# Linear attention and a rational FFN on one core: the first block of each batch as one chunk, the weight conversion's sign ahead of its shift, another order

## The chip, the cores and the metric

The kernel runs on one NeuronCore of a Trainium2 chip. PE (TensorE) does the matmuls, DVE (VectorE), ACT (ScalarE) and POOL (GpSimd) the elementwise work; SP (SyncE) issues all transfers between HBM and SBUF here. PE writes to PSUM, from where DVE and ACT read; POOL works on SBUF alone. The metric is the device time of one execution in microseconds, as the median of several runs. Beside it stands one profiled execution, whose trace gives start and duration of every instruction.

## The reference

The first half is a linear attention with a decaying state over 4 batches, 8 heads, 768 tokens and a head of 48; the second half is a feed-forward layer over 3072 tokens (384 to 2048 to 384) with a rational activation:

```python
for t in range(S):
    kt, vt, rt = (k[:, :, t], v[:, :, t], r[:, :, t])
    cur = np.einsum('bhd,bhe->bhde', u[None] * kt, vt)
    y[:, :, t] = np.einsum('bhd,bhde->bhe', rt, state + cur)
    state = w[None, :, :, None] * state + np.einsum('bhd,bhe->bhde', kt, vt)
...
h = x @ w_in
P = a[0] + a[1] * h + a[2] * h2 + a[3] * h3
Q = 1.0 + np.abs(b[0]) * np.abs(h) + np.abs(b[1]) * h2
return ((P / (Q + 1e-06)) @ w_out).astype(np.float32)
```

The decays w are drawn from 0.85 to 0.95. The FFN's weights come as 64-bit floats.

## The kernel before

**Attention.** The 24 blocks of 128 tokens are numbered n = 0 to 23; block n belongs to batch n % 4, so blocks 0 to 3 are the first of their batches. r and k are scaled with powers of the decay, so that the recurrence becomes matmuls. The scaling is centred on the middle of the block. For each block:

- "Lk", "Lr", "Lv" load, "sk" and "sr" scale; "ba", "bb", "bs", "bv" make the bonus term of u
- "tk" and "tr" transpose k and r on PE, "tke" and "tre" copy the results out of PSUM on ACT ("tre" in two halves)
- "a" (lines 542 to 551) makes the scores: the block is cut into two chunks of 64 tokens, and heads sit in pairs on the two row halves of the array, so that 64 × 64 matmuls alternate between the halves; "ae" applies the causal mask on DVE and puts the scores into the free half of the transposed r
- "kv" (564 to 575) makes the sums of k times v, once over the first 64 tokens and once over all 128; "kve" adds the state to them on DVE (for a first block, where there is none, it copies them on ACT)
- "LV" copies (ACT, DVE) or loads (SP) v into the state tile vs, beside the state, so that "y" (590 to 600) gets scores times v and r times state from one matmul of 128 rows and 64 columns of weights
- "ca" multiplies the state with the decay for the next block, "ye" adds the bonus, "x" transposes, "xh" and "xl" split the result into a high and a low FP32R part

**Weights.** The 28 pieces of w_in and w_out are loaded as integers ("cl"). ACT scales the top words ("c0") and the low words ("cu"); DVE shifts the scaled top words by 3 into a PSUM tile ("c2") and then puts the sign of the unshifted words on ("c3"); POOL adds the low word ("cr"); ACT rounds to the high part ("ch"), and POOL or DVE makes the low part ("co").

**FFN.** The hidden layer of 12 pairs of blocks is worked off in 50 slices, nearly all of four hidden tiles of 256 tokens. "f1" makes a slice (9 matmuls per hidden tile), ACT and DVE evaluate the activation ("z", "q", "t", "ln", "ex" on ACT, "u3", "hi", "p", "d", "lo" on DVE), "f2" multiplies with w_out, "os" evicts and "od" stores.

**Order.** All instructions of all engines are issued in the sequence of a long string, ORDER, written out by hand or by a search; a token names task, block or slice, engine and buffer (tke.0A: the copy of block 0's transposed k on ACT). Each engine works off its own tokens in that order. "warm" tokens are fill: matmuls of a constant tile with itself, whose result is not used:

```python
o_ = ops[max(ops)][1] if ops else idle_bank
nc.tensor.matmul(o_[:, DM:512], wones, wones, start=alone, stop=alone)
```

A test of the inputs at the end (the decays within W_MIN and W_MAX, among others) decides whether a slow general path runs behind the fast one.

Of the kernel before, what the change touches and what calls it, by code (L numbers as in the profile page):

```python
# [48 lines left out]
ORDER = """
pad.1G coefS wS Lv.2S plG uwS st0.1G st0.0G Lv.3S Lk.0S idG pad.0G pad.2G Lr.2S cl_D Lr.1S betaA sqD Lr.0S Lk.2S Lk.1S mskG ctrA  # L50
st0.3G st0.2A LV.1.1.1A LV.1.0.1A LV.1.0.0A LV.1.1.0A ubG warm.65P ubpPpa0 ubeA pow.0D turn.0.0Ppa1 pow.1D inv.1D pow.2D inv.2D
warm.20P turn.2.0P inv.0D wlD turn.1.0P tab.0A sr.1G sr.2D sr.0D warm.28P turn.0.1Ppa0 turn.1.1P turn.2.1P tab.1A sk.2D sk.0D
ba.2Dm0 ba.0Dm1 wpPpa1 w128A bb.2D sk.1G bs.2D bv.2D bb.0D tr.1Ph0 tre.1.0A tre.1.1A ba.1Gm2 bb.1G warm.16P tk.0Ppa0 tke.0A cl.2S
cu.2A c0.2A c2.2Dh1 c3.2D cr.2Gta0 Lv.0S cl.5S bs.0D bv.0G tr.0Ppa1 tre.0.1A tre.0.0A Lr.3S sr.3G kv.2Ph0 kve.2.0A kve.2.1A Lv.1S
kv.0Ppa0 Lk.3S sk.3G kve.0.0A kve.0.1A warm.14P a.0Ppa1 tk.1Ph1 tke.1A ae.0.1D ae.0.0D c0.5A c2.5Dh0 c3.5D warm.16P a.1Ph1
warm.10P tk.2Ph0 ae.1.0D ae.1.1D ch.2A co.2D LV.0.0.1A LV.0.1.0A LV.0.0.0A ba.3Dm3 bb.3D LV.0.1.1A warm.24P y.0Ph1 ca.0.0G ca.0.1G
cl.6S cu.6A c0.6A c2.6Dpa0 c3.6D cr.6Gta1 cl.12S cu.12A c0.12A tke.2A c2.12Dh0 Lr.4S sr.4G tr.2Ppa1 tre.2.1A tre.2.0A cl.1S c0.1A
bs.1D bv.1G Lk.5S cl.26S warm.17P kv.1Ppa0 kve.1.0A kve.1.1A Lk.4S kv.3Ppa1 kve.3.1A kve.3.0A cu.26A c3.12D cr.12Gta2 sk.5G ye.0D
warm.2P x.0Ph0 xh.0A bs.3D c2.1Dh1 c3.1D a.2Ppa0 tk.3Ppa1 tke.3A ae.2.1D ae.2.0D sk.4D y.1Ph1 tr.3Ppa1 ca.1.1D ca.1.0D ye.1D cu.5A
cr.5Gta3 xl.0D ba.4Dm1 bb.4G y.2Ppa0 ye.2D warm.37P x.2Ppa0 ch.12A Lr.5S sr.5G tre.3.1A c0.26A c2.26Dh1 c3.26D cu.1A cr.1Gta4  # L60
# [108 lines left out]
def tile_linear_attention_rational_ffn(ctx, tc, r, k, v, w, u, w_in, w_out, a, b, out):  # L169
# [65 lines left out]
    def pro_load():  # L235
        tab["zero"] = at.tile([P, P], F32, tag="os", name="zero", bufs=NO)
        nc.gpsimd.memset(tab["zero"], 0.0)
        nc.gpsimd.memset(identw, 0.0)
# [2 lines left out]
        nc.gpsimd.memset(wones, 1.0)
# [694 lines left out]
```

## Time and profile before

| | |
|---|---|
| median of 3 runs | 569.54 us (568.47 to 569.60) |
| profiled execution | 568.78 us, its span 567.1 us |
| PE / PEld busy | 550.2 / 528.6 us |
| DVE / ACT / POOL busy | 473.0 / 393.2 / 160.2 us |
| granted TensorE clock | 0.996 |

PEld is PE's weight load, which overlaps the matmuls. The span runs from the first to the last instruction; the time of an execution also holds what lies around it. A row of instructions names line, engine, operation, "output<-inputs" and the shape. "A <- B" in a view of waits says that A's engine sat idle until B was done. A matmul in FP32 appears as two instructions of PE.

### The profile page before, as it was taken

How to read it: one execution, taken by the hardware profiler on the slowest of the kernel's cores; microseconds unless marked ns; L12 is line 12 of the kernel's file. 1: busy time of each engine (PE TensorE's matmuls, PEld its weight loads, DVE VectorE, ACT ScalarE, POOL GpSimd, SP SyncE). 2: the span in 40 equal slices, each digit the busy share in tenths (PEclk: the TensorE clock that was granted, in tenths of full speed). 3: DMA queues.
4: the chain of work that ended last, by engine and by line, in shares of the span. 5: the costliest groups of instructions: out<-in, count | busy, mean ns of one | idle time of the engine just before them, and what ended most of it. 6: DMA issues, size and time to landing. Idle time of an engine off the chain costs nothing.

```text
span 567.1 us, 13844 instructions
## 1 busy us (share of the span) xinstructions
PE 550.2 (97%) x5934; PEld 528.6 (93%) x5934; DVE 473.0 (83%) x579; ACT 393.2 (69%) x516; POOL 160.2 (28%) x188
## 2 busy tenths in 40 slices
PE   7999999999999999999999999999999999999994
PEld 7889989899989999999999999999999999999983
DVE  6999998999998898888897878777788788867673
ACT  5899999876754846656577666577776666666762
POOL 5578677657324512331030001000130010000000
PEclk9999999999999999999999999999999999999998
DMA  9899901621244022240350012001010020000101
GB/s 145 217 266 258 297 2 21 152 49 22 44 84 79 16 44 59 61 85 16 57 99 12 18 21 58 1 1 43 1 44 1 1 64 1 1 15 1 68 4 34
DMA packets 96329, 34.89 MB, mean 62 GB/s; under 512 B 89602, under 2 KB 92676, under 8 KB 96260
## 3 DMA queue, kind: packets, MB, share of 16 engines
q1 hardware_dynamic: 96260, 33.93, 25.9%
q8 instruction: 48, 0.79, 0.6%
q14 instruction: 21, 0.17, 0.1%
HBM read 29.20 MB, written 4.72 MB: 60 GB/s over the span
## 4 chain that ended last, share of the span: by engine, by line
PE 55%; DVE 27%; ACT 11%; issue 3%; DMA 2%; POOL 1%; SPq 0%; DVEq 0%; ACTq 0%; POOLq 0%
PE h L643 21%; PE o L647 6%; PE o L649 6%; PE o L648 6%; DVE q L699 5%; DVE g L695 4%; DVE h L690 4%; DVE h L703 4%; PE y L599 4%; ACT z L682 3%; ACT z L686 3%; DVE l L708 3%; PE a L549 3%; PE idle_bank L796 2%; PE tr L526 2%
## 5 line engine op out<-in xcount | busy, mean ns | idle before, releaser
L643 PE MATMUL h<-xthi,wi 128*128 128x256 f32 x1152 | 216.0, 283 | 3.0 <-DVE l L708 3.0
L643 PEld LDWEIGHTS h<-xthi,wi 128*128 128x128 f32 x1152 | 179.8, 188 | 6.0 <-DVE l L708 2.6
L643 PE MATMUL h<-xtlo,wi 128*128 128x256 f32 x576 | 160.7, 279 | 0.0
L647 PE MATMUL o<-wo,g 128*128 128x384 f32 x384 | 131.5, 342 | 0.0
L649 PE MATMUL o<-wo,l 128*128 128x384 f32 x384 | 129.4, 337 | 1.0 <-DVE l L708 1.0
L648 PE MATMUL o<-wo,g 128*128 128x384 f32 x384 | 129.1, 336 | 0.0
L643 PEld LDWEIGHTS h<-xtlo,wi 128*128 128x128 f32 x576 | 108.4, 188 | 0.0
L695 DVE SCALAR_TENSOR_TENSOR g<-h,sig,z 128x1024 fp32r<-128x1024 f32 (+2 forms) x50 | 62.0, 1240 | 52.1 <-ACT z L686 51.6
L678 ACT ACTIVATE z<-h,off,root 128x1024 f32<-128x1024 f32 (+2 forms) x50 | 58.4, 1168 | 47.0 <-PE h L643 35.3
L682 ACT ACTIVATE z<-q,sig 128x1024 f32<-128x1024 f32 (+2 forms) x50 | 55.9, 1119 | 31.6 <-DVE h L690 30.8
L669 ACT ACTIVATE q<-h 128x1024 f32<-128x1024 f32 (+2 forms) x50 | 49.5, 989 | 36.8 <-PE h L643 23.7
L649 PEld LDWEIGHTS o<-wo,l 128*128 128x128 f32 x384 | 72.2, 188 | 1.5 <-DVE l L708 1.5
L647 PEld LDWEIGHTS o<-wo,g 128*128 128x128 f32 x384 | 72.2, 188 | 0.6 <-DVE g L695 0.2
L648 PEld LDWEIGHTS o<-wo,g 128*128 128x128 f32 x384 | 72.3, 188 | 0.0
L699 DVE SCALAR_TENSOR_TENSOR q<-q,sig,g 128x1024 f32<-128x1024 f32 (+2 forms) x50 | 66.2, 1324 | 1.8
L690 DVE SCALAR_TENSOR_TENSOR h<-z,sig,h 128x1024 f32<-128x1024 f32 (+2 forms) x50 | 62.0, 1240 | 5.5 <-ACT z L678 3.5
L703 DVE SCALAR_TENSOR_TENSOR h<-h,sig,q 128x1024 f32<-128x1024 f32 (+2 forms) x50 | 62.5, 1250 | 1.6
L708 DVE TENSOR_TENSOR l<-h,z 128x1024 fp32r<-128x1024 f32 (+2 forms) x50 | 59.1, 1182 | 3.5 <-DVE h L703 0.5
L673 ACT ACTIVATE q<-q,off,root 128x1024 f32<-128x1024 f32 (+2 forms) x50 | 60.4, 1209 | 1.2
L686 ACT ACTIVATE z<-z 128x1024 f32<-128x1024 f32 (+2 forms) x50 | 51.3, 1026 | 1.4
L521 POOL TENSOR_TENSOR m<-vn,dt 128x384 f32<-128x384 f32 x18 | 15.1, 840 | 120.6 <-DVE dt L517 116.9
L610 POOL TENSOR_TENSOR vs<-vs,w 48x192 f32<-48x192 f32 x32 | 20.3, 637 | 66.3 <-PE y L599 65.1
(137 smaller groups left out, 861.8 us busy)
## 6 DMA issues: line engine op xcount, KB each, us to landing
swi<-in_moe_w_in_dram SPq DMA_DIRECT2D x12, 512.0 KB, 7.9
swo<-in_moe_w_out_dram SPq DMA_DIRECT2D x16, 384.0 KB, 6.0
vn<-in_v_dram SPq DMA_DIRECT2D x24, 192.0 KB, 3.9
kh<-in_k_dram SPq DMA_DIRECT2D x24, 192.0 KB, 4.1
rh<-in_r_dram SPq DMA_DIRECT2D x24, 192.0 KB, 4.4
out_dram<-os SPq DMA_DIRECT2D x24, 192.0 KB, 2.4
vs<-in_v_dram SPq DMA_DIRECT2D x25, 96.0 KB, 3.5
coef<-in_moe_a_dram SPq DMA_DIRECT2D x1, 2.0 KB, 2.5
```

What stands on the lines that cost most here:

```text
L643: nc.tensor.matmul(o, wi_of(j, cc, part), x_[:, cc], start=(n == 0), stop=(n == 3 * NCC - 1))
L647: nc.tensor.matmul(o, hi, wo_of(j, HI), start=first, stop=False)
L648: nc.tensor.matmul(o, hi, wo_of(j, LO), start=False, stop=False)
L649: nc.tensor.matmul(o, lo, wo_of(j, HI), start=False, stop=last)
L673: nc.scalar.activation(g["q"], g["q"], AF.Square, scale=RB, bias=KB)
L682: nc.scalar.activation(g["z"], g["q"], AF.Ln, bias=QE)
L686: nc.scalar.activation(g["z"], g["z"], AF.Exp, scale=-1.0)
L690: nc.vector.scalar_tensor_tensor(g["h"], g["t"], KAP, g["h"], op0=ALU.add, op1=ALU.mult)
L695: nc.vector.scalar_tensor_tensor(g["hi"], g["h"], c0, g["z"], op0=ALU.add, op1=ALU.mult)
L699: nc.vector.scalar_tensor_tensor(g["q"], g["q"], qe, g["hi"].bitcast(F32), op0=ALU.add, op1=ALU.mult)
L703: nc.vector.scalar_tensor_tensor(g["h"], g["h"], c0, g["q"], op0=ALU.add, op1=ALU.subtract)
L708: nc.vector.tensor_mul(g["lo"], g["h"], g["z"])
```

## The change

1. The first block of each batch is treated as one chunk of 128 tokens without a state. Its scores are made at full width: for each row half (task "a.n.0" and "a.n.1") 4 matmuls with 64 rows, 128 columns of weights and 128 moving columns, masked on DVE into a tile of their own ("sc"). "kv" sums over the 128 tokens alone, 8 calls instead of 16. "y" multiplies the scores with v as it was loaded, 8 calls instead of 16, with 128 rows and 128 columns. The "LV" tasks of blocks 0 to 3 and the copies "kve" of the first blocks go; "ca" reads PSUM there, so it runs on DVE; "tre" is one copy there. The mask becomes a tile of 128 × 128.
2. The decay range for the fast path is 0.71 to 1.4 instead of 0.5 to 1.5.
3. "cs" masks the sign of the loaded top words into a PSUM tile (all 28 on DVE in this order), and "c2" then shifts the scaled words and puts that sign on. "c3" goes.
4. ORDER is another one from the first token to the last. It has 34 "warm" tasks with 450 matmuls instead of 27 with 457; ahead of slice 0 stand 369 instead of 316. Among the tasks that change their engine: "ba" 1 on DVE and 23 on POOL (8 and 16 before), "bb" 7 and 17 (12 and 12), "co" 2 and 26 (5 and 23), "ca" 19 and 21 (8 and 32), "LV" 6 on DVE, 13 on ACT, 21 on SP (3, 20, 25). Ahead of slice 0, POOL has 11 "cr", 5 "co", 4 "ba" and no "ca" (7, 2, 2 and 2 before).

```diff
-W_MIN, W_MAX = 0.5, 1.5
+W_MIN, W_MAX = 0.71, 1.4
...
 ORDER = """
-pad.1G coefS wS Lv.2S plG uwS st0.1G st0.0G Lv.3S Lk.0S idG pad.0G pad.2G Lr.2S cl_D Lr.1S betaA sqD Lr.0S Lk.2S Lk.1S mskG ctrA
+pad.2G cl.4S cs.4Dh0 c0.4A cl.12S wS c0.12A cl.5S pad.0G cu.12A plG mskG idG st0.3G cs.12Dpa0 c2.12D st0.2G cl.2S pad.1G cl_D ctrA
...
+        nc.gpsimd.memset(nought.bitcast(I32), SIGN)
         make_identity(nc, ident)
-        nc.vector.memset(ones, 1.0)
+        tab["ones"] = at.tile([1, P], F32, tag="os", name="ones", bufs=NO)
+        nc.vector.memset(tab["ones"], 1.0)
         nc.gpsimd.memset(wones, 1.0)
...
-    def cv_shift(c, p):
-        c["mag"] = pat("c2", p)[:, 0 : c["n"]].bitcast(I32)
-        nc.vector.tensor_scalar(c["mag"], c["top"], 3, None, op0=ALU.logical_shift_left)
-
-    def cv_sign(c):
-        nc.vector.scalar_tensor_tensor(c["top"], c["top"], SIGN, c["mag"], op0=ALU.bitwise_and, op1=ALU.bitwise_or)
+    def cv_sign(c, p, e):
+        c["sign"] = pat("cs", p)[:, 0 : c["n"]]
+        if e is nc.scalar:
+            e.activation(c["sign"], c["top"].bitcast(F32), AF.Identity, scale=0.0, bias=nought[:, 0:1])
+        else:
+            e.tensor_scalar(c["sign"].bitcast(I32), c["top"], SIGN, None, op0=ALU.bitwise_and)
+
+    def cv_shift(c):
+        nc.vector.scalar_tensor_tensor(c["top"], c["top"], 3, c["sign"].bitcast(I32), op0=ALU.logical_shift_left, op1=ALU.bitwise_or)
...
+    def trr_ev(n, e, half=None):
+        if half is None:
+            copy(e, rt.rearrange("p a t -> p (a t)"), state[n]["tr"])
+            return
...
+    def a_first(n, x):
+        p_ = state[n]["a", x] = pat("a", n, x)
+        for p in range(NP):
+            nc.tensor.matmul(p_[:, ts(p, P)], kt[ROWS[x], p], rt[ROWS[x], p], start=True, stop=True)
+
+    def a_first_ev(n, x):
+        if x == 0:
+            state[n]["sc"] = ew.tile([P, 2, NP, P], F32, tag=here[0], name=f"sc{n}")
+        av = state[n]["a", x].rearrange("p (a t) -> p a t", t=P)
+        nc.vector.tensor_mul(state[n]["sc"][:, x], av, mask.unsqueeze(1).to_broadcast([P, NP, P]))
+
+    def kv_first(n):
+        d = state[n]
+        d["kv"] = pv = pat("kv", n)[:, 0 : NP * D].rearrange("p (a d) -> p a d", a=NP)
+        for p in range(NP):
+            for x, o in enumerate((slice(0, D), slice(HALF, HALF + D))):
+                nc.tensor.matmul(pv[o, p], kh[n % 3][:, p, x, 0:D], d["v"][:, 2 * p + x], start=True, stop=True)
+
+    def carry_first(n, half):
+        dst, rows = ((0, slice(0, D)), (3, slice(HALF, HALF + D)))[half]
+        nc.vector.tensor_mul(vs[n][rows, dst], state[n]["kv"][rows], w128b[rows])
+
+    def y_first(n):
+        d = state[n]
+        d["y"] = pv = pat("y", n)[:, 0:DM].rearrange("p (h d) -> p h d", h=H)
+        for h in range(H):
+            nc.tensor.matmul(pv[:, h], d["sc"][:, h % 2, h // 2], d["v"][:, h], start=True, stop=True)
...
-        if i == 0:
-            copy(e, o, kv)
-        else:
-            nc.vector.tensor_add(
-                o, kv, s_[rows, prev : prev + 1].rearrange("p e a d -> p e (a d)").to_broadcast([D, 2, NP * D])
-            )
+        nc.vector.tensor_add(o, kv, s_[rows, prev : prev + 1].rearrange("p e a d -> p e (a d)").to_broadcast([D, 2, NP * D]))
```

More of the change, by code (lines that the diff above doesn't have):

```diff
@@ L53 @@
[L53 to L60, printed above, removed]
@@ new lines @@
+c2.4D cr.12Gta0 cs.5Dh1 coefS pow.0D warm.60P turn.0.0Ppa1 uwS st0.0G cu.5A cs.2Dpa0 ch.12A co.12G c0.5A c2.5D cr.5Gta1 betaA
+c0.2A Lr.0S ubG cu.4A cr.4Gta2 Lr.1S Lk.0S cl.0S pow.1D pow.2D inv.2D warm.40P turn.2.0P turn.1.0P tab.0A sr.1G sr.0G warm.14P
+ubpPpa1 ubeA inv.1D Lv.0S cl.10S inv.0D warm.18P turn.0.1Ppa1 turn.2.1P c2.2D Lk.1S Lv.1S cu.2A cr.2Gta3 turn.1.1P tab.1A wlD
+warm.10P wpPpa0 w128A tr.0Ph0 tre.0A sqD sk.0G ba.0Gm0 warm.15P kv.0Ppa1 ca.0.0D bb.0D tk.0Ppa0 tke.0A ca.0.1D sk.1D ba.1Gm1 bb.1G
@@ new lines @@
+co.26G lo.0Dta3 Lr.6S sr.6G z.1Ata4 q.1A sr.8G cl.16S y.5Ppa0 warm.18P tr.7Ppa1 ye.5D tre.7.0A tre.7.1A u3.1D warm.10P f2.0.0P
+ln.1A cs.9Dpa0 Lv.13S x.5Ppa1 cs.8Dh0 c2.8D cr.14Gta2 f2.0.1P xh.5A xl.5D f1.2.0Ph0 ex.1A cr.8Gta0 c2.9D cr.9Gta6 cl.7S c0.7A
+cu.7A os.0.0A hi.1Dta3 p.1D d.1D os.0.1A cl.23S tr.6Ppa1 ch.8A ch.9A co.9G tre.6.1A c0.16A f1.2.1P f1.2.2P f1.2.3P cs.7Dpa0
+lo.1Dta4 tre.6.0A c2.7D cu.16A z.2Ata6 sk.6G warm.7P tk.6Ppa1 t.2Ata5 cs.16Dh1 q.2A cs.23Dpa0 Lv.6S co.8G cr.7Gta0 ca.5.1G
@@ L198, in tile_linear_attention_rational_ffn @@
     ident = identw[:, D : D + P]
-    ones = cst.tile([1, P], F32, name="ones")
-    mask = cst.tile([P, HALF], F32, name="mask")
+    mask = cst.tile([P, P], F32, name="mask")
     wraw = cst.tile([P, NCC], F32, name="wraw")
@@ L211, in tile_linear_attention_rational_ffn @@
     wl = cst.tile([P, NCC], F32, name="wl")
+    nought = cst.tile([P, 1], F32, name="nought")
     wrn = cst.tile([P, H, D], F32, name="wrn")
@@ L244, in pro_mask @@
         nc.gpsimd.memset(mask, 1.0)
-        for rows in (slice(0, HALF), slice(HALF, P)):
-            nc.gpsimd.affine_select(
-                mask[rows], mask[rows], pattern=[[1, HALF]], base=-1, channel_multiplier=-1,
-                compare_op=ALU.is_ge, fill=0.0,
-            )
+        nc.gpsimd.affine_select(
+            mask, mask, pattern=[[1, P]], base=-1, channel_multiplier=-1, compare_op=ALU.is_ge, fill=0.0,
+        )
     def pro_coef():
@@ L294, in pro_spread @@
         tab["up"] = pat("pup")
-        nc.tensor.matmul(tab["up"][:, 0:DM], ones, tab["ur"].rearrange("o h d -> o (h d)"), start=True, stop=True)
+        nc.tensor.matmul(tab["up"][:, 0:DM], tab["ones"], tab["ur"].rearrange("o h d -> o (h d)"), start=True, stop=True)
     def pro_ub_all():
@@ L439, in tile_linear_attention_rational_ffn @@
     kt = cst.tile([P, NP, P], F32, name="kt")
+    rt = cst.tile([P, NP, P], F32, name="rt")
     for i in range(2):
@@ L560, in a_ev @@
         nc.vector.tensor_mul(
-            y_[rows].rearrange("p a (e t) -> p (a e) t", e=2), av, mask[rows].unsqueeze(1).to_broadcast([HALF, 2 * NP, HALF])
+            y_[rows].rearrange("p a (e t) -> p (a e) t", e=2), av, mask[rows, rows].unsqueeze(1).to_broadcast([HALF, 2 * NP, HALF])
         )
```

226 lines of the change are left out of this document (112 added, 114 removed).

## The prediction

> **What bounds the kernel now.** I read the page first: its opening line and the busy times of the engines.
>
> ```profile
> span 567.1 us, 13844 instructions
> PE 550.2 (97%) x5934; PEld 528.6 (93%) x5934; DVE 473.0 (83%) x579; ACT 393.2 (69%) x516; POOL 160.2 (28%) x188
> ```
>
> PE is busy 550.2 of 567.1 us. Since overlapping matmuls can make PE look busier than it is, I next cut the span into stages: up to the first FFN matmul, the rest of the weight conversion, and then four stretches of the FFN. The first cut comes from the group of the FFN's weight loads, whose first one starts at 49.2 us.
>
> ```profile
> L643 PEld LDWEIGHTS h<-xthi,wi x1152: 186/188/190, 49.2 to 554.7; 128*128 128x128 f32 x192
> ```
>
> ```profile
> core 0: us, PE busy (x) PEld busy (x) DVE busy (x) ACT busy (x) POOL busy (x), PEclk, DMA share, GB/s
> 0.00:49.20 49.20, 45.21 (x877) 41.16 (x877) 42.19 (x89) 39.59 (x89) 33.29 (x53) 1.00 0.92 227
> 49.20:102.80 53.60, 51.81 (x586) 49.88 (x582) 50.22 (x64) 50.63 (x76) 37.88 (x38) 1.00 0.51 125
> 102.80:204.00 101.20, 99.33 (x1138) 94.29 (x1139) 94.83 (x117) 70.10 (x94) 50.42 (x56) 1.00 0.28 57
> 204.00:300.00 96.00, 95.95 (x1184) 91.45 (x1182) 82.34 (x100) 60.37 (x74) 23.57 (x27) 1.00 0.32 60
> 300.00:532.00 232.00, 231.30 (x1989) 226.81 (x1988) 182.66 (x186) 155.25 (x161) 15.02 (x16) 1.00 0.06 17
> 532.00:567.10 35.10, 26.64 (x172) 24.96 (x170) 20.75 (x27) 17.31 (x25) 0.00 (x0) 0.93 0.12 42
> ```
>
> The columns are the stretch, its length, and the busy time (with the count) of PE, PEld, DVE, ACT and POOL. From 204 to 532 us PE is never free: 95.95 of 96.00 and 231.30 of 232.00. There the time is simply the sum of what PE is given. Before 102.8 us ACT (50.63 of 53.60) and DVE (50.22) are as full as PE, whose rows there hold fill matmuls: the order writes warm tasks into it, 457 single matmuls that compute nothing. What PE still loses to waits is in the view of waits, restricted to PE:
>
> ```profile
> engine line waited for: us in total, times, longest us
> PE h L643 <- DVE l L708: 3.0, 6, 1.0
> PE idle_bank L796 <- POOL wones L241: 2.4, 1, 2.4
> PE o L796 <- ACT os L755: 1.6, 3, 0.7
> PE tk L526 <- DVE swi L407: 1.0, 1, 1.0
> PE pup L295 <- POOL ur L290: 0.5, 1, 0.5
> ```
>
> Of PE's 16.9 us without work, 2.4 are the start, and 35.1 − 26.6 = 8.5 lie in the last stretch, most of them behind PE's last matmul. The waits that an order could remove are 3.0 + 1.6 + 1.0 + 0.5 = 6.1 us. So the change is worth what it takes out of PE's own list, plus or minus what it does to these waits. Work saved on another engine counts only through them.
>
> **PE's own list.** The timeline of PE gives a price for each kind of group. The rows below are starts; a group lasts until the next group's start.
>
> ```profile
> start us, us, engine line op out<-in xcount [idle before <-releaser]
> 15.91 0.24 PE L571 MATMUL kv<-vn,kh 64*48 64x48 f32 x1
> 16.41 0.24 PE L571 MATMUL kv<-vn,kh 128*48 128x48 f32 x1
> 16.91 0.23 PE L571 MATMUL kv<-vn,kh 64*48 64x48 f32 x1
> 22.36 0.27 PE L549 MATMUL a<-ysa,kt 64*64 64x64 f32 x1
> 23.44 0.73 PE L796 MATMUL idle_bank<-wones 128*128 128x128 bf16 x10
> 24.00 0.60 PE L526 MATMUL tk<-identw,kh 128*128 128x128 f32 x4
> 24.45 1.50 PE L796 MATMUL idle_bank<-wones 128*128 128x128 bf16 x24
> 25.88 0.32 PE L599 MATMUL y<-vs,ysa 128*64 128x48 f32 x4
> 26.95 0.66 PE L526 MATMUL tr<-identw,rh 128*128 128x128 f32 x4
> ```
>
> One kv of a block is a part on 64 rows (15.91 to 16.41, 0.50 us) and a part on 128 rows (16.41 to 16.91, 0.50). One a is 23.44 − 22.36 = 1.08 us for 32 matmuls of 64 columns. One fill matmul is (24.00 − 23.44)/10 = 0.056. One FP32 transpose with 128 columns of weights and 128 moving is (24.45 − 24.00)/4 = 0.11. One y is 26.95 − 25.88 = 1.07 for 32 matmuls of 64 columns of weights and 48 moving.
>
> *Fills.* The rows that price and count them, and one POOL memset for the start:
>
> ```profile
> L796 PEld LDWEIGHTS <-wones 128*128 128x128 bf16 x457 | 28.7, 102 | 5.2 <-POOL wones L241 2.4 <-issue 2.2
> L449 POOL MEMSET rh<- 128x128 f32 x3 | 0.6, 205 | 0.3 <-POOLq L920 0.3
> ```
>
> The new order has 34 warm tasks with 450 matmuls for 27 with 457: −7 × 0.056 = −0.4 us.
>
> *kv of the four first blocks.* The part on 64 rows goes: 4 × −0.50 = −2.0 us.
>
> *a of the four first blocks.* It becomes two tasks of 4 calls, 16 matmuls in all on 64 rows, with 128 columns of weights and 128 moving. The trace has no such matmul; the nearest is the transpose, 0.11 each: 1.76 us instead of 1.08, or +0.7. If the two row halves ran side by side, as the L549 and L550 pairs do now, it would be 0.88, or −0.2. Each task issues all its calls on one row half, so I take the upper end: 4 × 0.7 = +2.7 us, with −0.8 as the other end. The L549 and L550 rows would let one hope for the lower end; the Trainium skill ("TensorE: Matmul & The Clock Gate", Part 3: Packing small matmuls) speaks against it: only matmuls in different row groups run together, and they start in program order. By that rule the two halves can meet in one matmul at most.
>
> *y of the four first blocks.* 16 matmuls with 128 columns of weights and 48 moving. The row of the fill (128 columns of weights, 0.056) gives 0.90, the transpose gives 1.76, and 48/128 of a transpose gives 0.66. I take the fill, because with so few moving columns the weights should set the pace: 4 × (0.90 − 1.07) = −0.7 us, ends −1.6 and +2.8. The Trainium skill ("TensorEngine Tiling (Array Packing)", Key Properties) adds that a change of the tiling mode drains TensorE; the new y uses the whole array as the FFN does, so by that rule its edges would cost less, and the term would be nearer −1.6.
>
> *Start.* The first fill waits for the memset of wones on POOL. Ahead of it now stand two more memsets of a pad, at 0.2 each, and one small one: +0.4 us, ends 0 (if the fills merely shrink the next wait) and +0.6.
>
> The list together: −0.4 − 2.0 + 2.7 − 0.7 + 0.4 = 0.0 us. With the lower ends it is −4.8, with the upper ends +3.9. The planned idle time has not shrunk, and the attention's first blocks are no cheaper for PE.
>
> **Work off PE.** The rows of the copies on ACT, of the carry, and of the two conversion passes on DVE:
>
> ```profile
> L422 ACT COPY vs<-kv 48x384 f32<-48x384 f32 x8 | 3.7, 471 | 0.1
> L422 ACT COPY vs<-vn 64x192 f32<-64x192 f32 x40 | 12.0, 347 | 0.3
> L422 ACT COPY kt<-tk 128x512 f32<-128x512 f32 x24 | 14.0, 582 | 16.9 <-PE tk L526 16.9
> L610 DVE TENSOR_TENSOR vs<-vs,w 48x192 f32<-48x192 f32 x8 | 3.3, 418 | 0.1
> L404 DVE TENSOR_SCALAR c<-swo 128x384 int32<-128x384 int32 x16 | 8.8, 554 | 0.3 <-ACT swo L397 0.2
> L407 DVE SCALAR_TENSOR_TENSOR swo<-swo,c 128x384 int32<-128x384 int32 x16 | 8.7, 555 | 0.3
> ```
>
> ACT loses 8 copies of kv (8 × 0.47), 14 of its V copies (7 tasks fewer, 14 × 0.35) and four halves of a transposed copy (4 × 0.58): −11.0 us. Nearly all of that lies before slice 7 starts, in the stage where ACT is full. DVE gains 11 carries (11 × 0.42 = +4.6), the eight first ones now read PSUM; I price them by the SBUF row and leave −0.1 and +0.2 each as ends, at most +1.6 in all, hidden while DVE waits for ACT. DVE gives 12 bonus products and 3 low halves to POOL, each at least a pass of 384 columns (15 × 0.55 = −8.3), and gets a few small tasks back, so in all it ends 2 to 3 us lighter. In the order the two conversion passes on DVE stay 28 and 28. Masking the sign first is the same kind of pass (0.55 for 0.55); it only needs no scaled value, so it can run while ACT scales. That is one DVE pass less between landing and rounding, 0.55 us of latency for each weight piece, which costs nothing where ACT is the later one and has to be paid again if a sign tile holds its PSUM buffer longer than the shifted value did.
>
> **What that does to PE's waits.** The 1.6 us for the eviction belong to three fills that follow the last FFN-out matmul too closely; the new order has one such place: −1.0, ends −1.6 and 0. The 3.0 us for a late low half are DVE's lateness behind ACT. With ACT 11 us lighter I take half: −1.5, ends −3.0 and +3.0 (as many new ones). The wait of a transpose for DVE's conversion (1.0): its new buffer is freed by another DVE pass, so half, −0.5, ends −1.0 and +1.0. Against this stand waits that a wholly new order brings: nothing in the trace shows them; the ends are 0 and the 6.1 of the list over again; I take 1.5, a quarter, since the FFN's part keeps its pattern. Together −1.5 us.
>
> The profiled execution took 568.8 us, 1.7 around its span, and lies 0.8 below the median of the runs shown, 569.5, within their spread (568.5 to 569.6). The difference −1.5 is carried over to the median: **568.0 us**. What is within 0.2% (1.1 us) can hardly be told from no change here.
>
> **The rivals.** *All the waits go.* The list stays at 0.0, and ACT's 11 us remove the full 6.1: 569.5 − 6.1 = 563.4 us. For it: ACT and DVE are the full engines before 102.8 us. Against it: after 204 us only 0.7 + 0.05 us of PE are free, so any gain must come earlier.
>
> *No change.* The fills were laid for the idle time expected, and the new order holds nearly as many: list 0.0, old waits replaced by new ones of the same size: 569.5 us. Against it: ACT's relief must show somewhere.
>
> *POOL becomes the bound of the prologue.* The rows:
>
> ```profile
> L610 POOL TENSOR_TENSOR vs<-vs,w 48x192 f32<-48x192 f32 x32 | 20.3, 637 | 66.3 <-PE y L599 65.1
> L507 POOL TENSOR_TENSOR m<-rh,kh 128x384 f32<-128x384 f32 x16 | 16.4, 1028 | 30.9 <-PE x L618 29.3 <-DVE rh L503 0.8
> L411 POOL TENSOR_TENSOR bwo<-swo 128x384 int32<-128x384 int32 x16 | 13.7, 854 | 3.0 <-ACT swo L400 1.6 <-ACT swi L397 1.1 <-DVE swo L407 0.2
> L411 POOL TENSOR_TENSOR bwi<-swi 128x512 int32<-128x512 int32 x12 | 12.4, 1040 | 5.5 <-DVE swi L407 2.4 <-ACT vs L422 2.3 <-PE o L649 0.3
> L419 POOL TENSOR_TENSOR wo<-bwo,wo 128x384 fp32r<-128x384 f32 x14 | 14.2, 1016 | 12.8 <-ACT wo L416 10.5 <-DMA swi<-in_moe_w_in_dram 2.3
> ```
>
> Ahead of slice 0 the new order gives POOL 4 more roundings (about 0.9 each), 3 more low halves (1.0), 2 more bonus products (1.0) and 2 fewer carries (0.64): 3.6 + 3.1 + 2.1 − 1.3 = +7.5 us on 33.3. PE's own list ahead of slice 0 grows by 53 fills (3.0) and the start (0.4), so slice 0 would start near 52.6 us, and POOL's idle time before it shrinks from 15.9 to 52.6 − 40.8 = 11.8 us. POOL issues in order, so its waits for landings are paid one after another, with the low half of piece 0 last. If nothing of the 7.5 is absorbed, PE waits 7.5 − 3.4 = 4.1 us; with 2.5 of it the time is 569.5 + 2.5 = 572.0 us. It decides once slice 0 starts later than about 53.7 us. A second row bears on it:
>
> ```profile
> L699 DVE SCALAR_TENSOR_TENSOR q<-q,sig,g x50: 464/1285/2316, 63.8 to 558.1; 128x1024 f32<-128x1024 f32 x47, 128x256 f32<-128x256 f32 x2, 128x512 f32<-128x512 f32 x1
> ```
>
> The same instruction takes 1.29 us in the middle and up to 2.3, so something can hold DVE for 1.0 us. If each of the 12 moved products did that once, DVE would lose 12 us against the 8.3 it sheds, +3.7, and the time would be 573.2 us at most. The Trainium skill ("SBUF — State Buffer", SBUF: two separate sides) names what could: GpSimd and a DVE operation with two SBUF inputs shut each other out for a whole instruction.
>
> *The change doesn't do what it says*: if a decay lay outside 0.71 to 1.4, the whole general path would run behind the fast one. The decays are drawn from 0.85 to 0.95, so I give it no chance.
>
> **Chances.** A small gain, as forecast, 0.30 (its own range 565.5 to 569.0; 0.25 of it beyond 0.2%); all the waits go, 0.20; no change, 0.25; POOL bound or dear new matmuls, 0.25. That makes faster 0.45, same 0.30, slower 0.25. The range runs from 562.5 (the waits gone and a little of the list's lower end) to 573.0 (POOL's 4.1 less a little, or the list's upper end of +3.9).
>
> **What would show it.** Right: the new a group about 1.8 us and y about 0.9 in PE's timeline; kv 0.5; ACT busy 382 us in all; slice 0 at 52 to 53.5 us; PE's waits for L708 and the eviction at about 2 us together; PE still full after 204 us. Wrong: slice 0 after 53.7 us with POOL the releaser, a y near 1.8 us, or PE's waits in the middle unchanged near 6 us. A time under 565 would mean that PE's list itself became shorter than I count.

## The result, and the profile after

The changed kernel takes **575.72 us** (median of 4 runs, 574.51 to 576.91), and the kernel before, timed beside it, 569.0 us (568.46 to 569.6): a ratio of 1.0119, 95% interval 1.0103 to 1.0136. It is slower by 6.7 us; the prediction said 568.0 us and a range up to 573.0. The profiled execution of the changed kernel took 576.91 us with a span of 575.2; its span is 8.1 us longer than that of before. It is the slowest of the four; the fastest, at a mean granted clock of 0.997, is still 5.5 us slower than the kernel before. One run of an experiment below (581.41 us, of kh_on_dve) lies over 1.5% above the fastest of its kernel and is left out of the comparisons.

The page of the changed kernel begins so:

```profile
span 575.2 us, 13391 instructions
PE 555.4 (97%) x5735; PEld 534.5 (93%) x5735; DVE 474.1 (82%) x582; ACT 383.4 (67%) x490; POOL 167.6 (29%) x191
```

ACT is lighter by 9.8 us (393.2 before), near the 11.0 of the forecast, and the kernel is slower all the same. DVE is 1.1 us heavier (473.0 before), where 2 to 3 us lighter was forecast. PE has 199 matmul instructions fewer (5934 before; a matmul in FP32 is two) and is busy 5.2 us longer (550.2 before). That can come from dearer matmuls or from a slower clock, and the view of windows, restricted to PE, separates the two. Columns: stretch, length, PE busy (count), granted clock, DMA share, GB/s. First the kernel before:

```profile
core 0: us, PE busy (x), PEclk, DMA share, GB/s
10.00:25.00 15.00, 14.03 (x280) 1.00 0.90 201
90.00:100.00 10.00, 10.00 (x120) 1.00 0.25 47
```

And the changed kernel:

```profile
15.00:20.00 5.00, 3.58 (x63) 0.96 0.67 134
20.00:25.00 5.00, 5.00 (x53) 0.70 0.66 121
25.00:59.20 34.20, 33.76 (x492) 1.00 0.83 226
90.00:100.00 10.00, 7.74 (x50) 0.83 0.39 94
```

There are two holes. Each has a stretch in which PE waits (3.58 busy of 5; 7.74 of 10) and a granted clock below 1.00 in it or right behind it: 0.70 from 20 to 25 us, 0.83 over 90 to 100 us. In the kernel before both stretches run at 1.00. PE's waits in the changed kernel name the holes (columns: total us, times, longest):

```profile
engine line waited for: us in total, times, longest us
PE idle_bank L827 <- POOL wones L243: 2.7, 1, 2.7
PE o L827 <- ACT os L786: 2.3, 1, 2.3
PE ptab L344 <- DVE pw L313: 2.0, 2, 1.7
PE o L680 <- DVE l L739: 1.5, 2, 0.8
PE pwp L333 <- DVE wl L323: 1.4, 1, 1.4
PE h L674 <- DVE l L739: 0.7, 1, 0.7
```

The early hole is the decay chain: PE waits for the scanned powers `pw` (2.0) and for `wl` (1.4). The later one is a fill (`L827`) that writes into the PSUM bank of an output which ACT has yet to evict (`os`, 2.3 us in one piece; before, 1.6 in three). The waits for the late low half `l` did fall, from 3.0 + 1.0 to 0.7 + 1.5.

The dear matmuls stand in PE's timeline (start, busy, what; a group lasts until the next one's start):

```profile
start us, us, engine line op out<-in xcount [idle before <-releaser]
25.52 0.56 PE L567 MATMUL kv<-vn,kh 128*48 128x48 f32 x16
26.01 0.23 PE L827 MATMUL idle_bank<-wones 128*128 128x128 bf16 x1
28.74 1.71 PE L554 MATMUL a<-rt,kt 64*128 64x128 f32 x16
30.38 0.79 PE L827 MATMUL idle_bank<-wones 128*128 128x128 bf16 x11
37.52 1.94 PE L577 MATMUL y<-vn,sc 128*128 128x48 f32 x16
39.29 0.50 PE L827 MATMUL idle_bank<-wones 128*128 128x128 bf16 x6
```

A first block's kv is 0.49 us (about 1.0 before), its a 1.64 (1.08 before), its y **1.77** (1.07 before). Over four blocks that is −2.0, +2.2 and +2.8 us; with 7 fills fewer (−0.4) PE's own list grew by 2.6 us.

So the 8.1 us of the span can be accounted for: PE is idle 2.9 us longer (19.8 for 16.9) and busy 5.2 us longer. Of the 5.2 the list has 2.6, and the rest fits an estimate of the slower clock from the two windows: 0.30 of 5.00 us and 0.17 of 7.74 us are 2.8.

Slice 0 begins at 59.2 us instead of 49.2. Summing PE's groups up to there: fills with the waits in front of them and among them grew from 21.2 us (316) to 28.5 (369), y from 4.3 to 7.2, a from 6.2 to 8.2, and kv fell from 6.0 to 4.1. PE is busy 33.76 of the last 34.2 us ahead of slice 0 and waits there for another engine only once, 0.4 us for a mask. Since part of that work is fills, a full PE doesn't by itself show that PE sets the start; half_fills, below, bears on it. Of the 10.0 us 8.1 are left at the end. Fifty-three fills (3.0 us) only moved ahead of slice 0, which may be why, but no run shows it.

### The profile page after: what moved, and what is told of

Its sections match the earlier page's. It is cut to its first block, busy times and chain, and to the rows that moved or that the text cites. A ratio compares the mean times of both kernels' runs of the same rounds, so it can differ in the third digit from the quotient of the medians.

```text
span 575.2 us, 13391 instructions
## 1 busy us (share of the span) xinstructions
PE 555.4 (97%) x5735; PEld 534.5 (93%) x5735; DVE 474.1 (82%) x582; ACT 383.4 (67%) x490; POOL 167.6 (29%) x191
## 4 chain that ended last, share of the span: by engine, by line
PE 69%; DVE 19%; ACT 7%; issue 3%; DMA 1%; SPq 0%; POOL 0%; ACTq 0%; DVEq 0%
PE h L674 27%; PE o L678 8%; PE o L680 8%; PE o L679 8%; DVE g L726 3%; DVE q L730 3%; PE a L586 3%; DVE h L721 3%; PE y L631 3%; DVE h L734 3%; PE kv L608 3%; ACT z L713 3%; PE idle_bank L827 3%; ACT z L717 2%; PE tk L530 2%
## 5 line engine op out<-in xcount | busy, mean ns | idle before, releaser
L674 PE MATMUL h<-xthi,wi 128*128 128x256 f32 x1152 | 220.6, 285 | 1.2 <-DVE l L739 0.7
L674 PEld LDWEIGHTS h<-xthi,wi 128*128 128x128 f32 x1152 | 182.2, 189 | 4.1 <-DVE l L739 1.1
L730 DVE SCALAR_TENSOR_TENSOR q<-q,sig,g 128x1024 f32<-128x1024 f32 (+2 forms) x50 | 62.7, 1255 | 1.9
L525 POOL TENSOR_TENSOR m<-vn,dt 128x384 f32<-128x384 f32 x16 | 13.5, 842 | 114.2 <-DVE dt L521 97.5
L827 PEld LDWEIGHTS <-wones 128*128 128x128 bf16 x450 | 29.4, 104 | 7.3 <-issue 3.6
```

The lines of the kernel that those rows point to most:

```text
L674: nc.tensor.matmul(o, wi_of(j, cc, part), x_[:, cc], start=(n == 0), stop=(n == 3 * NCC - 1))
L730: nc.vector.scalar_tensor_tensor(g["q"], g["q"], qe, g["hi"].bitcast(F32), op0=ALU.add, op1=ALU.mult)
```

## The experiments

All were timed in five rounds beside the kernel before, whose median was 568.6 to 568.8 us in each of the four groups of runs. The changed kernel itself was not timed again: "less than the changed kernel" compares with its 575.72 us, whose four runs spread over 2.4 us, so a difference of 2 us from it is weak evidence by its time alone. The theory from the two traces: the loss is made of pieces with a place each, namely y, the fills that wait for the eviction, and the decay chain. Its rival: the searched order is slower as a whole, and no few pieces bring it back.

**y in halves of the columns.** The change calls y with 128 columns of weights, once for each head; here it is two calls of 64.

```
-            nc.tensor.matmul(pv[:, h], d["sc"][:, h % 2, h // 2], ...)
+            for c in ROWS:
+                nc.tensor.matmul(pv[c, h], d["sc"][:, h % 2, h // 2, c], ...)
```

> The changed kernel with the y of the first blocks made in two column halves: 16 calls with 64 columns of weights instead of 8 with 128; same values, same order. Theory A (the changed kernel's loss is what PE's own list gained, plus waits and a slow clock in the prologue): a first-block y falls from 1.77 us to about 1.1, four times 0.65 = 2.6 us, so about 573.1 us against 575.7, a ratio to the kernel before of about 1.007. Theory B (POOL and the late weights set the start of slice 0, PE's list before it is cover): y falls too, but slice 0 stays at 59 us and the time at 575.7, ratio 1.012.

Measured: 573.63 us, ratio 1.009 (1.0069 to 1.0111), 2.1 us less than the changed kernel. The two intervals overlap, so the trace has to carry the reading: the 32 instructions of 16 calls take 1.07 us in place of the 1.77 of 16 instructions of 8 calls (35.62 to 36.69 in the profile):

```profile
35.62 1.14 PE L578 MATMUL y<-vn,sc 128*64 128x48 f32 x32
```

Twice the calls, 0.70 us less. The halves write different halves of PSUM's partitions and run side by side: in the trace the two instructions of a pair start 0.006 us apart, and pairs follow each other every 0.058 us, where the single instructions of the changed kernel follow every 0.112. Slice 0 starts at 55.3 us in this profile (59.2 in the changed kernel), so the start does depend on PE's list or on its clock, which was 1.00 here from 15 to 25 us; the two are not separated.

**a with its row halves issued in turn.** The two matmuls of a head pair use rows 0 to 63 and 64 to 127 of the array; the change issues all of the first half and then all of the second.

```
         for p in range(NP):
-            nc.tensor.matmul(p_[:, ts(p, P)], kt[ROWS[x], p], rt[ROWS[x], p], ...)
+            for z in range(2):
+                nc.tensor.matmul(state[n]["a", z][:, ts(p, P)], kt[ROWS[z], p], rt[ROWS[z], p], ...)
```

> The changed kernel with the two score tasks of a first block issued together, their calls alternating between the two row halves of the array; for block 2 the first task moves down to the second, for the others only the masks move. Theory A: the row halves run side by side, 16 matmuls in 0.9 to 1.0 us instead of 1.64, four times 0.7 = 2.7 us less, about 573.0 us, ratio 1.007. Rival (full-width FP32 matmuls of the two halves don't overlap): 1.64 us as before and 575.7. Theory B (POOL sets the start of slice 0): a shorter, the time still 575.7.

Measured: 578.75 us, ratio 1.0186 (1.0146 to 1.0226), slower than the changed kernel by 3. The group itself became 1.09 us in place of 1.64 (the instructions of the two halves start 0.006 us apart, pairs every 0.112), but PE then waits for DVE's masks. In block 1 DVE makes them no earlier than in the changed kernel. Its timeline there, first the changed kernel and then this run:

```profile
31.22 1.29 DVE L560 TENSOR_TENSOR sc<-a,mask 128x512 f32<-128x512 f32 x2
```

```profile
31.70 1.29 DVE L565 TENSOR_TENSOR sc<-a,mask 128x512 f32<-128x512 f32 x2
```

The scores were done at 30.38 and at 28.44. In both runs DVE comes to the masks straight from other work, so PE only arrives earlier and waits for a DVE that is full. Waits and windows of PE in this run:

```profile
PE tr L532 <- DVE sc L565: 3.4, 2, 2.8
35.00:40.00 5.00, 5.00 (x52) 0.71 0.31 113
```

A gain of 2.2 us in PE's list was paid for with 3.4 us of waiting (0.4 in the changed kernel) and, in the profile, a clock of 0.71 behind it.

**Without the fills ahead of slice 3.**

```
-... os.1.1A ch.16A warm.2P f1.3.0Ph1 ...
+... os.1.1A ch.16A f1.3.0Ph1 ...
```

> The changed kernel without the one fill of 2 matmuls that stands between the last matmul of FFN-out of slice 1 and the first of slice 3. Theory A: that fill waited 2.3 us for the eviction of the bank it writes, and slice 3 behind it ran at a lower granted clock (5.94 us instead of 4.3); both go, 2.3 + 1.6 = 3.9 us, about 571.8 us, ratio 1.005. Rival (slice 3 would wait as long for its weights or its inputs): 575.6, ratio 1.012, with the wait now at slice 3.

Measured: 571.46 us, ratio 1.0056 (1.0037 to 1.0075). Two matmuls that compute nothing, 0.11 us of work, cost **4.3 us**, more than their wait of 2.3. In the profile of the changed kernel a slower clock stood behind that wait, but behind the same wait of 2.2 to 2.3 us the clock stayed at 1.00 in the profiles of y_half, decay_first and kh_on_dve; so which share of the 4.3 us the clock has is open. In PE's windows the hole is closed:

```profile
90.00:100.00 10.00, 9.84 (x128) 1.00 0.49 108
```

**The decay chain earlier.** The load of w goes first in its queue, and the scans of the powers ahead of the conversion's passes on DVE.

```
-pad.2G cl.4S cs.4Dh0 c0.4A cl.12S wS ... plG ... cl_D ctrA ... pow.0D ... pow.1D pow.2D ... wlD
+pad.2G wS cl.4S cs.4Dh0 c0.4A cl.12S plG cl_D ctrA pow.0D pow.1D pow.2D wlD
```

> The changed kernel with the load of the decay vector first in the queue, and the clamp, the powers and the last power on DVE ahead of the second conversion piece; the fills stay. Theory A: PE's waits for the powers (2.0 us) and for the last power (1.4 us) go, and with them the slow clock between 20 and 25 us (about 1.5): 3.4 to 4.9 us, about 571.5 us, ratio 1.005. Rival (what is late next takes their place: the scaled r and k of POOL, or the landings behind the first weight pieces): less than 1 us, 575, ratio 1.011.

Measured: 576.59 us, ratio 1.0143 (1.0119 to 1.0167): no gain. The waits for the powers are gone, and the next thing that is late, GpSimd's product for u, holds PE instead; the clock falls behind it. Waits and windows of PE:

```profile
PE pup L297 <- POOL ur L292: 3.0, 1, 3.0
15.00:20.00 5.00, 5.00 (x63) 0.60 0.55 92
```

**The parts of the change alone, on the kernel before.** First, the sign: `cs` masks it into PSUM, `c2` then shifts, and in 11 pieces `cs` is moved ahead of `c0`, ACT's scaling of the same piece. One of them:

```
-cl.6S cu.6A c0.6A c2.6Dpa0 c3.6D cr.6Gta1
+cl.6S cu.6A cs.6Dpa0 c0.6A c2.6D cr.6Gta1
```

> The kernel before with the sign masked first and then the shift, and nothing else: in 11 of the 12 pieces where ScalarE's copy of the low bits stood just ahead, the mask is moved ahead of that copy. Theory A (the same two passes over the same piece, 0.55 us less latency): no change, ratio 0.998 to 1.002. Rival B (the sign mask in the old place of the shift holds the shared buffer longer or shorter and moves the late low half of 3.0 us): ratio below 0.997 or above 1.003.

Measured: **583.97 us**, ratio 1.0266 (1.0241 to 1.0292). Theory A fell, and B's bound was passed, but not for its reason: 15 us for an order that I had priced at nothing. The scaling writes the piece in place and may not start until the mask has read it, so ACT now waits for DVE. ACT's waits up to 62 us, of which the kernel before has none in its list:

```profile
ACT swo L400 <- DVE cs L407: 6.4, 5, 2.9
ACT swi L400 <- DVE cs L407: 4.4, 2, 3.2
```

Behind those scalings stand ACT's copies for attention and its evictions, and PE waits for them:

```profile
PE o L799 <- ACT os L758: 5.9, 3, 5.0
PE a L552 <- ACT ysa L425: 3.1, 1, 3.1
```

The control leaves each mask behind its scaling, where the shift stood.

> The kernel before with the sign masked first and then the shift, and every instruction in its old place: the mask stands where the first shift stood, behind ScalarE's scaling of the piece. It differs from sign_alone only in that 11 masks are not moved ahead of the scaling. Theory A (the two passes cost what the old two cost, and sign_alone lost its 15 us because ScalarE's scaling, which writes the piece in place, then had to wait for VectorE's mask, 10.8 us in 7 waits): no change, 568.6 us, ratio 0.998 to 1.002, and no wait of ScalarE for a mask. Rival B (the swap itself costs, by the mask's or the shift's duration or its shared buffer): ratio 1.01 or more.

Measured: 568.59 us, ratio 1.0007 (0.999 to 1.0024). The swap costs nothing; the order of mask and scaling does. In the changed kernel's order seven masks stand ahead of their scalings, and ACT waits 5.7 us for three of them. So the opposite was tried there: the scaling first in these seven pieces.

```
-cs.5Dh1 coefS pow.0D warm.60P turn.0.0Ppa1 uwS st0.0G cu.5A cs.2Dpa0 ch.12A co.12G c0.5A
+c0.5A cs.5Dh1 coefS pow.0D warm.60P turn.0.0Ppa1 uwS st0.0G cu.5A c0.2A cs.2Dpa0 ch.12A co.12G
```

> The changed kernel with ScalarE's scaling put ahead of VectorE's mask in the 7 pieces (2, 4, 5, 6, 10, 13, 23) where the searched order has the mask first. Theory A (those masks cost ScalarE 5.7 us of idle time in three waits ahead of slice 0; ScalarE is full from 62 to 95 us, so what it lost is missing at the eviction behind slice 1, for which TensorE waits 2.3 us and then runs at 0.73 of its clock): the wait for the eviction shrinks, 572 to 574 us, ratio to the kernel before 1.006 to 1.010, and the wait of ScalarE for a mask is gone. Rival B (the first of the three waits, 2.6 us at 2.1 to 4.7, and most of the rest lie where ScalarE had nothing to do): unchanged, 575 to 577 us, ratio 1.011 to 1.014. Rival C (the scalings moved forward stand ahead of copies that TensorE waits for, and wait themselves for their pieces to land): above 577 us.

Measured: 582.37 us, ratio 1.0218 (1.0187 to 1.0248), rival C. The scalings now stand in front of what PE needs: the eviction's wait grew from 2.3 to 3.8 us, and a wait behind a late mask of a, with a clock of 0.52, came new. Waits and windows of PE:

```profile
PE o L829 <- ACT os L788: 3.8, 1, 3.8
PE tr L532 <- DVE sc L562: 2.9, 1, 2.9
35.00:40.00 5.00, 5.00 (x39) 0.52 0.33 119
```

ACT's 5.7 us were a cost that the rest of that order was built around, and not one to be taken out by itself.

Second, the first block in the old order; ca on DVE takes the place of ACT's evictions of kv, and a second score buffer is taken from those that were free.

```
-kv.0Ppa0 ... kve.0.0A kve.0.1A ... a.0Ppa1 ... ae.0.1D ae.0.0D ... LV.0.0.1A ... y.0Ph1 ca.0.0G ca.0.1G
+kv.0Ppa0 ... ca.0.0D ca.0.1D ... a.0.0Ppa1 a.0.1Ppa0 ... ae.0.0Dta5 ae.0.1D ... y.0Ph1
```

> The first block of each batch as one chunk of 128 tokens, alone, in the order of the kernel before: the sign is still masked after the shift, the evictions and fills stand where they stood, and of the searched order nothing is taken over. Theory A (what the change loses in its first block is TensorE's list, the rest comes from the order): the list grows by 4 x 0.70 (y) + 4 x 0.56 (a) - 4 x 0.50 (kv) = +3.0 us and the waits of the kernel before stay, so the time is about 571.8 us against 568.7 before, ratio 1.005 (1.003 to 1.008). Rival B (the lighter ScalarE, 11 us less copying ahead of slice 7, pays wherever the order is the old one): the 1.6 us wait for the eviction and the 3.0 us wait for the low half go, the time is 568 us or less, ratio at most 1.000. Rival C (the first block in itself brings the waits that were put down to the order): 574 us or more, ratio 1.009 or more.

Measured: 595.15 us, ratio 1.0451 (1.0423 to 1.048).

> The same as first_alone with the two matmul groups in their cheaper form: y in two halves of 64 columns of weights (1.07 us instead of 1.77 per block), a with the two row halves issued in turn (1.09 instead of 1.64). Theory A (list alone): +3.0 - 2.8 - 2.2 = -2.0 us against the kernel before, 566.7 us, ratio 0.9965 (0.994 to 0.999). Rival C (a group of a in turn needs both score buffers at once, and the masks on VectorE come late as they did in the changed kernel's order, 3.4 us): 569.5 us or more, ratio 1.001 to 1.006.

Measured: 589.21 us, ratio 1.0343 (1.0309 to 1.0377). Both are nearest to rival C, by far more than it said. One place of the stall is the queue of loads. v is now read until y, where the old y read a copy of it in the state tile and v's buffer came free earlier, so in first_half SP stands still for 15.7 us on one load of v, with k and r of the next blocks behind it. PE runs dry, and then runs at half its clock; PE's windows in first_half:

```profile
20.00:25.00 5.00, 1.12 (x10) 0.80 0.00 0
25.00:30.00 5.00, 5.00 (x42) 0.52 0.02 5
35.00:40.00 5.00, 0.38 (x7) 1.00 0.89 233
```

A fourth buffer for v tests that.

```
-            t, src = ld.tile([P, H, D], F32, tag="ldv", name=f"vn{n}"), v
+            t, src = ld.tile([P, H, D], F32, tag="ldv", name=f"vn{n}", bufs=4), v
```

> first_half with four buffers for the loads of v instead of three. In the first-block form v is read until y, where the kernel before was done with it at kv; in first_half the queue of loads stood still for 15.7 us on the load of v that needed the buffer that y frees, and k and r of the next blocks stood behind it. Theory A (that standstill is the largest part of the 20 us by which first_half is slower, through waits of 7.0 us at kv and a clock of 0.50 behind them): the queue's wait for y is gone, the time falls by 10 us or more to 579 us or less, ratio below 1.018; what is left above 1.000 is the wait for VectorE's scaling of the state (5.0 us) and the clock behind it. Rival B (the masks and the scaled state on VectorE set the pace, the loads are late only because everything is): less than 3 us are gained, 586 us or more.

Measured: 580.51 us, ratio 1.0199 (1.0174 to 1.0224): 8.7 us less, most of theory A's 10 and far from rival B's 3. The longest wait that is left is DVE's scaling of the state, 5.0 us, again followed by a slow clock (0.53 from 25 to 30 us); waits of 1.8 and 0.8 us come later, with a second slow stretch (0.50) behind 35 us. With waits of such a size these three runs can't say what the list alone costs in the old order; that stays open.

```profile
PE a L554 <- DVE vs L571: 5.0, 1, 5.0
```

**Half of all fills.** Each group of the changed kernel's fills at half its count.

```
-warm.60P turn.0.0Ppa1 ... warm.40P turn.2.0P ... warm.10P wpPpa0
+warm.30P turn.0.0Ppa1 ... warm.20P turn.2.0P ... warm.5P wpPpa0
```

> The changed kernel with each of its fill groups at half its count (about 225 fills fewer of 450, 56 ns each, 12.6 us of TensorE's list). Theory A (most fills stand where TensorE would wait anyway for data of the prologue; a few delay what is ready): the time falls by 2 to 5 us, mostly by the fills ahead of slice 3 and those behind slice 5, to 571 to 574 us, and the idle time of the profile grows by 8 to 11 us. Rival B (the fills are all dead work in front of ready data): the time falls by about 12 us to 563 us. Rival C (the longer idle stretches lower the granted clock as the waits of 2 to 3 us did): the clock in the slices from 10 to 60 us shows 0.6 to 0.8 in several windows and the time rises above 577 us.

Measured: 574.09 us, ratio 1.0093 (1.0062 to 1.0125), just outside theory A's span. PE has 220 matmuls fewer (12.3 us of fills) for a gain of 1.6 us. So most of what the fills take is no loss by itself: without them it turned into waits and, early on, a halved clock (the two aren't separated):

```profile
5.00:10.00 5.00, 1.43 (x15) 0.87 1.02 255
10.00:15.00 5.00, 4.70 (x30) 0.50 0.93 224
15.00:20.00 5.00, 5.00 (x49) 0.50 0.66 124
```

**The pieces together.** First the cheaper y and no fills ahead of slice 3.

> The changed kernel with y_first in two halves of 64 columns and without the two fills that wait for the eviction ahead of slice 3. Each alone gave 2.1 and 4.3 us. Theory A (they act at different places, 26 to 45 us and 91 to 96 us, so they add up): 569.3 us, ratio 1.001 (0.999 to 1.003). Rival B (slice 0 comes earlier with the cheaper y and ScalarE, full from 62 to 95 us, is then the bound behind slice 1 with or without the fills): 571 us or more, ratio 1.004 or more.

Measured: 571.03 us (12 runs, 569.05 to 574.46), ratio 1.0028 (1.0013 to 1.0043): between the two theories, 1.7 us above the plain sum. The runs differ, and so does their clock: 574.46 us at a mean clock of 0.988, 569.05 at 0.996. The profiled one is the slowest of them; its one long wait in the decay chain and PE's windows behind it:

```profile
PE ptab L346 <- DVE pw L315: 2.6, 2, 2.0
15.00:20.00 5.00, 5.00 (x36) 0.53 0.39 75
20.00:25.00 5.00, 5.00 (x62) 0.50 0.26 51
```

If the pause is the clock's cause, PE must be kept busy there while the data stay late: 45 more fills.

```
-warm.60P turn.0.0Ppa1 ... warm.40P turn.2.0P ... warm.10P wpPpa0
+warm.75P turn.0.0Ppa1 ... warm.52P turn.2.0P ... warm.28P wpPpa0
```

> y_no_fill with 45 more fills at the places of the decay chain at which TensorE waits (15 ahead of the first turned power, 12 ahead of the second, 18 ahead of the small matmuls pwp): 2.5 us of matmuls that compute nothing, in front of data that are late anyway. The data come when they came. Theory A (the pauses cost twice: the pause itself, and a clock of 0.50 to 0.70 in the 5 to 10 us behind it, which made one execution of y_no_fill 574.5 and another 569.1 us): with TensorE busy the clock stays 1.00 from 10 to 25 us, the mean clock is 0.996 or more in every execution, the time 569.0 us, ratio 0.9995 to 1.002, and the spread of the runs is smaller. Rival B (the granted clock has nothing to do with the pauses, or comes from something else in the prologue): clock and time as in y_no_fill, ratio 1.003, or more by the fills that come too late (up to 1.5 us).

Measured: **569.16 us** (12 runs, clocks 0.996 to 0.998), ratio 0.9996 (0.9977 to 1.0016). More work that computes nothing made the kernel 1.9 us faster than y_no_fill. About 1.3 of these lie inside the span (medians 567.4 for 568.65); the rest is what lies around it. The two intervals just touch, so the clock in the windows and the smaller spread of the runs carry the reading:

```profile
15.00:20.00 5.00, 5.00 (x101) 1.00 0.77 168
20.00:25.00 5.00, 5.00 (x73) 1.00 0.66 120
```

With three small edits the changed kernel is level with the kernel before, so the rival, the order as a whole, falls. Slice 0 still starts 5.9 us later than before (55.1 for 49.2): its start alone doesn't set the total.

To go below, a's row halves in turn in blocks 1 and 3, where the two halves are neighbours anyway:

> busy_pause with the row halves of a issued in turn in blocks 1 and 3, whose two halves stand next to each other in the order anyway; in blocks 0 and 2, where a_pairs made VectorE's masks late, they stay as they are. Theory A (the list loses 2 x 0.55 us, nothing new waits): 1.1 us less than busy_pause, ratio 0.997 to 1.000, two groups of a at 1.09 us. Rival B (the first half's mask, which could start half a group earlier before, is late as in a_pairs): no gain against busy_pause or a loss, with a wait behind the masks.

Measured: 569.14 us, ratio 0.9988 (0.9968 to 1.0008): no gain on busy_pause. The groups take 1.09 us, and PE waits for a mask in their place. That is rival B's result, but not its reason: the scores of block 1 end earlier (27.86 for 28.68 in busy_pause), and DVE, at other work until then, comes to the masks at 30.15 (29.56):

```profile
PE tr L532 <- DVE sc L569: 1.9, 1, 1.9
```

**GpSimd and VectorE.** In the changed kernel a DVE multiplication of 3 columns took 2.21 us, and it stands ahead of `pwp` in the decay chain. DVE's and then GpSimd's timeline:

```profile
15.54 2.21 DVE L323 TENSOR_TENSOR wl<-pw,sq 128x3 f32<-128x3 f32 x1
```

```profile
15.74 1.03 POOL L414 TENSOR_TENSOR bwi<-swi 128x512 int32<-128x512 int32 x1
16.74 0.99 POOL L503 TENSOR_TENSOR kh<-kh,wkn 128x384 f32<-128x384 f32 x1
```

It ends at 17.75, just behind GpSimd's second operation (17.73). The experiment puts that second operation on DVE, behind `wl`:

```
-tab.1A wlD warm.10P ... sqD sk.0G
+tab.1A wlD sk.0D warm.10P ... sqD
```

> The changed kernel with the scaling of k of block 0 on VectorE, behind the small multiplication wl, instead of on GpSimd. In the changed kernel wl, 128x3 elements, took 2.21 us while GpSimd worked through an addition (1.02 us) and this scaling (0.99). Theory A (VectorE's operations on two SBUF operands stand still while GpSimd's run): wl takes about 1.2 us, TensorE's wait at pwp falls from 1.4 to at most 0.5 us, the time by 1 us or more (clock behind the pause), 574.5 us or less. Rival B (wl was late for another reason, its duration in the record is not work held by GpSimd): wl stays at 2 us or more and the time at 575 to 577 us.

Measured: 575.25 us (nine runs, 572.58 to 579.79), ratio 1.0104 (1.007 to 1.0137). The mechanism held: `wl` took 1.25 us and ended at 16.09, just behind the one GpSimd operation left beside it (16.07), and the wait at `pwp` fell to 0.5:

```profile
14.84 1.25 DVE L325 TENSOR_TENSOR wl<-pw,sq 128x3 f32<-128x3 f32 x1
```

In y_no_fill, where GpSimd was idle beside it, `wl` took 0.16 us. The time did not move by what theory A said (574.5 us or less). In the profile PE waits 1.4 us for a late mask a little later, and the clock falls there instead (0.69 and 0.63 from 30 to 40 us). The 2.21, 1.25 and 0.16 us agree with the Trainium skill ("SBUF — State Buffer", SBUF: two separate sides), by which a DVE operation with two SBUF inputs and a GpSimd operation that reads SBUF shut each other out for a whole instruction.

**The kernel before without its fills that wait for an eviction.**

```
-warm.33P f2.1.0P ... os.1.1A warm.5P tk.6Ppa0 ... lo.3Dta4 warm.16P f1.5.0Ph1
+f2.1.0P ... os.1.1A tk.6Ppa0 ... lo.3Dta4 f1.5.0Ph1
```

> The kernel before without the three groups of fills (33, 5 and 16) at which TensorE waits 1.6 us for an eviction on ScalarE. Theory A (as in the changed kernel, where two such fills cost 2.3 us and a slower clock: a fill writes into the bank that the eviction frees, so the fill itself brings the wait): 1 to 3 us less, 566 to 567.7 us, ratio 0.995 to 0.998. Rival B (at these places the data behind the fills are late as well, ScalarE and VectorE are full there): no change, ratio 0.999 to 1.001, with the waits for VectorE's low half grown by as much.

Measured: **567.36 us** (12 runs), ratio 0.9967 (0.9947 to 0.9987), faster than both kernels. Fifty-four fills fewer (3.0 us) gave 1.4 us; the eviction's wait fell from 1.6 to 0.7, and the waits for the late low half grew from 4.0 to 5.8:

```profile
PE h L645 <- DVE l L710: 3.8, 6, 1.0
PE o L651 <- DVE l L710: 2.0, 2, 1.0
PE o L798 <- ACT os L757: 0.7, 1, 0.7
```

## Why the prediction was wrong, step by step

The steps that held. *The frame*: what is worth something is what changes PE's list and PE's waits; ACT's 9.8 us didn't show in the time. *kv* −2.0 forecast, −2.0 measured. *Fills* −0.4, as in the trace. *Start* +0.4 forecast, +0.3 measured (2.4 to 2.7 us). *a*: +2.7 forecast from the transpose row, +2.2 measured. *The late low half*: −1.5 forecast, 4.0 to 2.2 measured. *The transpose's wait for the conversion*: −0.5 forecast, and its 1.0 us left PE's list of waits. For DVE the forecast had the wrong sign (2 to 3 us lighter; 1.1 heavier), but no step of the sum used it.

The steps that failed. The list was forecast at 0.0 and grew by 2.6 us; the waits were forecast to fall by 1.5 us, while PE's idle time grew by 2.9 and slower clocks, which no term of the sum held, came on top:

- **Waits, eviction (−1.0 forecast).** I read the fills' wait for the eviction as a small leak that a lighter ACT would close. It is the fill itself that waits, since it writes into the bank; the new order put one where ACT is full. In place of falling, the wait grew from 1.6 to 2.3 us (with 0.6 more for an eviction on DVE), and in the profile a lower clock followed it. Measured with no_fill: 4.3 us.
- **y, a term that was mis-sized.** Between a fill (0.056 us, 128 columns of weights, bf16) and a transpose (0.11, 128 columns of weights, FP32) I took the fill. The rate followed the transpose: 0.110 an instruction, +2.8 us in place of −0.7. The upper end of that term was exact, and the sentence on the mode change, which pointed to its lower end, has no support in these runs. Measured with y_half: the group falls back from 1.77 to 1.07 us and the kernel's time by 2.1, with the same arithmetic. The right row was the one with the same type and the same columns of weights.
- **New waits (+1.5 forecast).** The pauses of the decay chain alone sum to 3.4 us in the changed kernel, and a slower clock behind them was not in the forecast at all. Measured with busy_pause against y_no_fill: 1.9 us (1.3 inside the span) for pauses that were only filled, not shortened.
- **"Sign first, cost 0".** True for the two passes (sign_behind 1.0007), wrong for the edit as it is used in an order. The prediction says that the mask can run while ACT scales; it can't, since the scaling writes the piece in place. Ahead of the scaling the mask ties ACT to DVE: 15 us in sign_alone, 5.7 us of ACT's time in the changed kernel. What these 5.7 us alone cost there could not be isolated, since moving the scalings forward cost more.
- **What I had not listed**: v is held until y. It stops the queue of loads for 15.7 us in first_half. In the changed kernel that queue also waits for y, and no run shows whether PE pays for it.

Two slips of the working decided nothing: the upper ends of the list sum to +3.7 and not to +3.9, and the view from which the 6.1 us of waits were taken has three more of PE's rows, 1.8 us together. The bound of 53.7 us for slice 0 stands there without a working.

Taken out one after the other, the pieces lead back: 575.7, then 571.0 without the dear y and the eviction's fills, then 569.2 with PE busy in the decay chain, against 568.8 before.

**Of the rivals**, the line of chances named "POOL bound or dear new matmuls", and its second half is a part of what happened (a and y, +5.0 us). The first half (GpSimd bounds the prologue, 572.0 us) had the right sign and the wrong place: slice 0 came at 59.2 us, far behind its 53.7, but PE was busy in front of it, with fills, y and a, and no wait for GpSimd stands there. Its second row, GpSimd holding DVE, was real (2.21 us for 3 columns; 1.25 with one of the two GpSimd operations gone), and removing half of it moved no time that these runs could tell. The rule of the Trainium skill that I cited for a ("TensorE: Matmul & The Clock Gate", Part 3: Packing small matmuls) fits both forms: half by half only three instructions of the second half start beside one of the first and the group takes 1.64 us, and in turn the row halves run together (1.09).

**Of what should have shown it**: kv at 0.5 and ACT at 382 (383.4) were right, a at 1.64 near its 1.8, y at 1.77 was named there as the sign of a wrong step and was one. Waits of `l` and eviction "about 2" were 1.5 + 0.7 + 2.3.

## What to carry to other kernels

Price a new matmul by the row with the same type and the same number of weight columns, and where outputs can be split over partitions or rows, try the narrow calls issued in turn: here twice the calls took 40% less time. Where PE must wait for something early, try whether filling the wait pays, as it did in busy_pause, and look first whether the fill itself waits for a buffer. An in-place pass makes every reader ahead of it a wait for the engine that writes, so when two cheap passes change places, look at what must now wait for which, and which queue stands behind it.
